# Squares by GpSimd in one leg of a fused attention and feed-forward kernel, and weight rows split earlier

## The chip, the cores and the metric

The kernel runs on one core of a Trainium2 chip. The metric is the device time of one launch in microseconds (us), the median of several runs. A profiled execution gives the trace; its span is the time from the first to the last instruction. Engines: TensorE does the matrix products (PE; PEld for its weight loads), VectorE is DVE, ScalarE ACT, GpSimd POOL, and SyncE (SP) issues the DMAs.

## The reference

Attention with a sink and a window, then a feed-forward layer with squared ReLU (named "moe" in the code, with one expert):

```
scores = q @ k.T / 8                     # 4 batches, 8 heads, 768 positions, head size 64
keep   = (key < 4) or (0 <= query - key < 128)
a      = softmax(where(keep, scores, -1e9))
x      = (a @ v), heads side by side     # 3072 x 512
h      = max(x @ w_in, 0)                # 512 x 2048
out    = (h * h) @ w_out                 # 2048 x 512, float32
```

The weights arrive as float64.

## The kernel before

**Chunks and pairs.** The 3072 tokens form eight chunks of 384 tokens (two a batch), `c` = 0 to 7. Each chunk has four pairs of heads. Attention of a pair makes scores (PE), the masked maximum and exponent (DVE L266, ACT L269), the scaling of the probabilities (GpSimd, `normalise`), transposes (PE, copied by ACT or DVE into PTF), and the values (PE, `xo`), which become x as a high and a low part (ACT L401, DVE L402).

**Precision.** Each float32 operand of the feed-forward products stands as two float32r tiles, high and low, and a product is three products: high·high, low·high, high·low. A weight row (128 x 512 float64) is loaded raw and split into such a pair: `split_steps` runs five DVE instructions (L540, L542, L544, L546, L553), an ACT copy of the low half-words (L539) and an ACT copy that makes the high part (L552). There are NROW = 32 rows, in an order that interleaves four groups of four rows of w_in and four of w_out; HALF is 16. Raw rows take turns in four buffers, and each split issues the load of the row two ahead.

**Legs of products.** `moe` walks through legs (chunk, first and last block of d_ff). Chunks 0 and 1 go through blocks 0 to 7 first (legs 1 and 2), then through 8 to 15 (legs 3 and 4); all other chunks take 16 blocks at a time. For each block, PE adds up 12 products into the PSUM tile `ph` (L448), ACT makes r = ReLU(ph) (L456) and gh = r² rounded to float32r (L459), and DVE makes the square in full (L461, in place in `ph`) and its low part gl = square − gh (L465). While that happens PE does the second products of the block before, nine with 512 columns (L478). The generator yields four times a block; one such step is a quantum. At the end of a leg, `evacuate` copies or adds three PSUM tiles (L496 to L506) and stores them.

**The order.** Leg 1, with the attention of chunks 0 and 1 and the splits of rows 0 to 15, is written out by hand: in that section each engine's instructions keep the program's order. `fill(n)` there does n steps of the splits (five steps make a row), up to HALF rows. From leg 2 on a planner orders each engine's instructions by priority and by its own cost estimates, and moves work ahead where an engine would idle. What it is given is program order: in each leg, `plan` says up to which unit of attention the leg goes, from which row to which row the splits go, and over which share of the leg (the last number). Rows are also split early enough for the blocks that need them (`need`). Leg 2 has no attention units, leg 3 has 24. A split counts as 10 places less urgent than its place in the program.

**Buffers that matter.** `r` has one buffer, `gh` and `gl` two, `ph` two PSUM banks. The probabilities of attention ("P", pool `ap4`) have four buffers of 128 x 792 float32.

Of the kernel before, what the change touches and what calls it, by code (L numbers as in the profile page):

```python
# [8 lines left out]
F32 = mybir.dt.float32  # L9
# [5 lines left out]
ALU = mybir.AluOpType  # L15
# [3 lines left out]
P = 128  # L19
# [4 lines left out]
TOK = 384  # L24
# [11 lines left out]
def f32(ap):  # L36
    return ap.bitcast(F32)
# [3 lines left out]
def sink_window_attention_moe(  # L41
# [11 lines left out]
    nc = tc.nc  # L53
    B, NPAIR, _, S = q.shape
# [12 lines left out]
    with ExitStack() as fast:  # L67
# [5 lines left out]
        ap4 = fast.enter_context(tc.tile_pool(name="ap4", bufs=4))  # L73
# [76 lines left out]
        def wi_at(i, cc, fc):  # L150
            f0 = fc * P
            return wi[:, cc, f0 // WR, i, f0 % WR : f0 % WR + P]
# [81 lines left out]
        def bank(tag, name):  # L234
            pool = {"att": ps_att, "h": ps_h, "xo": ps_x}.get(tag, ps_o)
            return pool.tile([P, 512], F32, tag=tag, name=name)
# [199 lines left out]
        def moe(legs):  # L436

            items = [(c, f0, f1, fc) for c, f0, f1 in legs for fc in range(f0, f1)]
            squares = {}
            for n in range(len(items) + 1):  # L440
                if n < len(items):
                    c, f0, f1, fc = items[n]
                    xh, xl = xT[c]
                    ph = ps_h.tile([P, 512], F32, tag="h", name=f"ph_{c}_{fc}")
                    m = 0
                    for cc in range(NCC):
                        for i, xt in ((0, xh), (1, xh), (0, xl)):
                            nc.tensor.matmul(  # L448
                                ph[:, 0:TOK], wi_at(i, cc, fc), xt[:, cc, :],
                                start=(m == 0), stop=(m == 3 * NCC - 1),  # L450
                            )
                            m += 1
                        if cc % 2 == 1 and cc < NCC - 1:
                            yield
                    r = ap1.tile([P, TOK], F32, tag="r", name=f"r_{c}_{fc}")
                    nc.scalar.activation(r, ph[:, 0:TOK], AF.Relu)  # L456
                    gh = mp.tile([P, TOK], F32R, tag="gh", name=f"gh_{c}_{fc}")
                    gl = mp.tile([P, TOK], F32R, tag="gl", name=f"gl_{c}_{fc}")
                    nc.scalar.activation(gh, r, AF.Square)  # L459
                    yield  # L460
                    nc.vector.tensor_tensor(ph[:, 0:TOK], ph[:, 0:TOK], r, op=ALU.mult)  # L461
                    squares[n] = (gh, gl)
                late = None
                if n < len(items):
                    late = lambda: nc.vector.tensor_tensor(gl, ph[:, 0:TOK], f32(gh), op=ALU.subtract)  # L465
                if n == 0:
                    yield
                    late()
                    yield
                    continue  # L470
                c, f0, f1, f = items[n - 1]
                ghp, glp = squares.pop(n - 1)
                if f == f0:
                    po = [ps_o.tile([P, DM], F32, tag=f"o{t}", name=f"po_{c}_{f0}_{t}") for t in range(NQ)]
                for t in range(NQ):
                    ts_ = slice(t * P, (t + 1) * P)
                    for j, (gt, i) in enumerate(((ghp, 0), (ghp, 1), (glp, 0))):
                        nc.tensor.matmul(  # L478
                            po[t], gt[:, ts_], wo[f][:, i, :],
                            start=(f == f0 and j == 0), stop=(f == f1 - 1 and j == 2),  # L480
                        )
                    if t == 1:
                        yield
                        if late:
                            late()
                if f == f1 - 1:
                    evacuate(c, f0, f1, po)
                yield
# [26 lines left out]
        NROW = len(order)  # L515
        HALF = NROW // 2
# [62 lines left out]
        split = []  # L579

        def row_steps():
            for n in range(NROW):
                yield from split_steps(n)
                split.append(n)
                yield

        FH = NFC // 2
        legs = [(0, 0, FH), (1, 0, FH), (0, FH, NFC), (1, FH, NFC)] + [(c, 0, NFC) for c in range(2, NCHUNK)]
        products = moe(legs)
        QUANTA = 4 * FH  # L590
        with tc.manual_schedule(engines={E.PE, E.DVE, E.Activation, E.Pool, E.SP}):
            steps = row_steps()

            def fill(n):
                for _ in range(n):
                    if len(split) < HALF:
                        next(steps)

            def scores(s, i, tags=("att", "att")):
                for hh in range(2):  # L600
                    score(*pairs[s], hh, i, tags[hh])

            def busy(n):

                t = bank("o2", "idle")
                for _ in range(n):
                    nc.tensor.matmul(t, idle[:, 0:P], idle, start=True, stop=True)

            def tail(s, spare):

                a = pairs[s]
                probs(*a, 0)
                if s == 0:
                    busy(10)
                yield
                sink_keys(*a, spare[0])
                probs(*a, 1, spare[1])
                yield
                probs(*a, 2)
                yield  # L620

            load_qk(*pairs[0])
            load_row(0)
            load_qk(*pairs[1])
            load_row(1)
            load_v(*pairs[0]), load_v(*pairs[1])
            load_row(2)
            split_sinks = load_sinks(0)
            busy(7)

            for s in range(NPAIR + 1):
                if s > 0:
                    load_qk(*pairs[s + 1])
                for i, tags in enumerate((("att", "att"), ("h", "h"), ("o0", "o1"))):
                    scores(s, i, tags)
                    fill(1)
                fill(1)

                normalise(*pairs[s], (0, 1))
                if s == 1:  # L640
                    split_sinks()
                if s < 2:
                    busy(4 + 4 * s)
                rest = values(*pairs[s - 2], True) if s > 1 else None
                if s > 0:
                    if s > 1:
                        load_v(*pairs[s])
                    t = tail(s - 1, ("o2", "h"))
                    next(t)
                    fill(1)  # L650
                    if rest:
                        rest()
                    next(t)
                    fill(1)
                    next(t)
                else:
                    fill(1)
            rest = values(*pairs[NPAIR - 1], True)
            fill(2)
            rest()  # L660

            todo = []
            for s in range(NPAIR + 1, 2 * NPAIR + 1):
                if s < 2 * NPAIR:
                    todo += [lambda s=s: (s + 1 < 2 * NPAIR and load_qk(*pairs[s + 1]), scores(s, 0))]
                    todo += [lambda s=s, i=i: scores(s, i) for i in range(1, NQ)]
                    todo += [lambda s=s: normalise(*pairs[s], (0, 1))]
                else:
                    todo += [lambda: values(*pairs[s - 2])]
                if s > NPAIR + 1:  # L670
                    todo += [lambda s=s: values(*pairs[s - 2])] if s < 2 * NPAIR else []
                t = tail(s - 1, ("att", "att"))
                todo += [lambda t=t: next(t)] * 3
                if s < 2 * NPAIR:
                    todo.append(lambda s=s: load_v(*pairs[s]))
            todo.append(lambda: values(*pairs[2 * NPAIR - 1]))
            for n in range(QUANTA):
                next(products)
                fill(2 if n < QUANTA // 2 and n % 3 or n % 4 == 0 else 1)
                if todo:  # L680
                    todo.pop(0)()
            while len(split) < HALF:
                next(steps)
            for f in todo:
                f()
        nrow = len(split)
# [7 lines left out]
        units, ready = [], [0, 0]  # L694
# [37 lines left out]

        LEAD = 2.5

        plan = [(ready[1], HALF, 24, 1.0), (ready[1] + 24, 24, NROW, 0.9), (ready[2], NROW, NROW, 1.0)]
        plan += [(ready[min(c + 1, NCHUNK - 1)], NROW, NROW, 1.0) for c in range(2, NCHUNK)]
        flag = None
        checked = 0
# [219 lines left out]
```

## Time and profile before

| what | us |
|---|---|
| median of 3 runs (713.13 to 715.03) | 713.21 |
| profiled execution: time | 712.63 |
| profiled execution: span | 710.9 |
| PE busy | 691.0 |
| DVE busy | 486.1 |
| ACT busy | 392.6 |
| POOL busy | 236.4 |

The profile counts an engine as busy while one of its instructions runs; matrix products are pipelined, so a busy PE isn't PE at its peak. In the tables by stage a row has the stretch, its length, and for each engine its busy time with the number of instructions in brackets, then the granted PE clock as a share of full speed, the share of time in which the DMA engines work, and GB/s. A line of a timeline has start, duration, engine, source line, operation and tiles. A group of instructions has count, busy time, mean in ns, then the idle time before them. A wait has the waiting engine and line, what ended the wait, and the total in us, the number of times and the longest.

### The profile page before, as it was taken

The numbers are of one execution on the slowest core, as the hardware profiler recorded it, in microseconds if no ns is written. First come the engines' busy times: TensorE is split into PE (matmuls) and PEld (weight loads), VectorE is DVE, ScalarE is ACT, GpSimd is POOL, SyncE is SP. The second block draws the span as 40 slices with busy tenths as digits, with TensorE's granted clock in tenths as the row PEclk, the third lists the DMA queues.
The fourth block names the chain that finished last, engine by engine and source line by source line (L and its number), as shares of the span: only waits on it lengthen the run. The fifth ranks groups of instructions, "written<-read, shape, count | busy, mean of one in ns | idle before, by whom it ended". The sixth has DMA issues, their size and how long they took to land.

```text
span 710.9 us, 11803 instructions
## 1 busy us (share of the span) xinstructions
PE 691.0 (97%) x3895; PEld 597.2 (84%) x3895; DVE 486.1 (68%) x1275; ACT 392.6 (55%) x1075; POOL 236.4 (33%) x435
## 2 busy tenths in 40 slices
PE   8889999999999999999999999999999999999995
PEld 4567789988878988888898888889888898889995
DVE  8998789996788766665766776665666766542232
ACT  5887666754455666665666666566666443322221
POOL 6655300063455334423324443432443333200000
PEclk9999999999999999999999999999999999999998
DMA  8575345531524433243343523343332310001001
GB/s 241 166 232 168 119 155 175 195 93 27 164 59 129 131 98 102 62 130 106 87 118 103 152 76 94 90 136 109 100 90 83 92 43 16 1 3 43 1 1 49
DMA packets 37013, 71.78 MB, mean 101 GB/s; under 512 B 4368, under 2 KB 14096, under 8 KB 36944
## 3 DMA queue, kind: packets, MB, share of 16 engines
q1 hardware_dynamic: 36944, 70.95, 33.7%
q8 instruction: 33, 0.54, 0.3%
q14 instruction: 36, 0.29, 0.1%
HBM read 63.06 MB, written 7.86 MB: 100 GB/s over the span
## 4 chain that ended last, share of the span: by engine, by line
PE 86%; DVE 6%; ACT 4%; issue 1%; DMA 1%; SPq 1%; DVEq 0%; ACTq 0%
PE po L478 35%; PE ph L448 35%; PE xo L390 6%; PE s L262 4%; PE pt L360 2%; PE xo L393 2%; ACT P L269 1%; PE s L258 1%; PE pss L307 1%; DMA raw<-in_moe_w_in_dram 1%; PE pt L342 1%; DVE gl L465 1%; ACT m L539 1%; DVE ph L461 1%; DVE rs L279 1%
## 5 line engine op out<-in xcount | busy, mean ns | idle before, releaser
L448 PE MATMUL ph<-x,wi 128*128 128x384 f32 x1536 | 306.6, 340 | 0.0
L448 PEld LDWEIGHTS ph<-x,wi 128*128 128x128 f32 x1536 | 265.3, 188 | 8.0 <-issue 1.4
L478 PE MATMUL po<-wo,gh 128*128 128x512 f32 x768 | 244.1, 398 | 0.4 <-DVE ob L497 0.4
L230 POOL TENSOR_TENSOR KS<-kn,KS 128x408 fp32r<-128x408 f32 (+1 forms) x48 | 72.0, 1500 | 330.6 <-DVE KS L229 315.8
L478 PE MATMUL po<-wo,gl 128*128 128x512 f32 x384 | 151.5, 395 | 0.3 <-DVE gl L465 0.3
L478 PEld LDWEIGHTS po<-wo,gh 128*128 128x128 f32 x768 | 135.6, 188 | 18.9 <-issue 1.4
L269 ACT ACTIVATE P<-P,nbs 128x264 f32<-128x264 f32 (+1 forms) x192 | 94.6, 493 | 79.0 <-DVE nbs L266 73.1
L456 ACT ACTIVATE r<-ph 128x384 f32<-128x384 f32 x128 | 62.7, 490 | 111.6 <-PE ph L448 110.9
L461 DVE TENSOR_TENSOR ph<-ph,r 128x384 f32<-128x384 f32 x128 | 71.6, 559 | 63.6 <-ACT r L456 62.7
L266 DVE CUSTOM_DVE_ANT_0 P<-s,masks 128x264 f32<-128x264 f32 x160 | 67.2, 429 | 59.3 <-PE s L262 56.3
L291 POOL TENSOR_SCALAR P<-P,rs 128x136 f32<-128x136 f32 (+2 forms) x192 | 84.2, 454 | 28.6 <-DVE rs L280 13.7
L478 PEld LDWEIGHTS po<-wo,gl 128*128 128x128 f32 x384 | 72.1, 188 | 16.7 <-DVE gl L465 0.8
L465 DVE TENSOR_TENSOR gl<-ph,gh 128x384 fp32r<-128x384 f32 x128 | 71.0, 555 | 10.2 <-DVE ph L461 0.5
L459 ACT ACTIVATE gh<-r 128x384 fp32r<-128x384 f32 x128 | 67.2, 525 | 3.5
L262 PE MATMUL s<-KS,QS 128*128 128x264 f32 (+1 forms) x288 | 57.1, 281 | 0.2
L262 PEld LDWEIGHTS s<-KS,QS 128*128 128x128 f32 x288 | 51.8, 188 | 5.9 <-DVE nbs L266 1.5
L366 DVE TENSOR_TENSOR PTF<-pt,halves 128x256 f32<-128x256 f32 x96 | 36.2, 419 | 22.5 <-PE pt L360 22.0
L279 DVE TENSOR_SCALAR rs<-sm 128x3 f32<-128x3 f32 (+1 forms) x56 | 48.5, 866 | 3.0 <-ACT P L269 1.6
L390 PE MATMUL xo<-PTF,vn 128*64 128x256 f32 x448 | 47.3, 348 | 2.5 <-ACT PTF L349 2.5
L286 POOL TENSOR_TENSOR P<-P 128x256 f32<-128x256 f32 (+1 forms) x48 | 42.9, 894 | 16.7 <-ACT P L269 16.7
L390 PEld LDWEIGHTS xo<-PTF,vn 128*64 128x64 f32 x448 | 31.9, 138 | 19.3 <-issue 9.5
L401 ACT CAST x<-xo 128x384 fp32r<-128x384 f32 x32 | 15.3, 478 | 55.7 <-PE xo L393 55.7
(97 smaller groups left out, 645.9 us busy)
## 6 DMA issues: line engine op xcount, KB each, us to landing
raw<-in_moe_w_in_dram SPq DMA_DIRECT2D x16, 512.0 KB, 4.5
raw<-in_moe_w_out_dram SPq DMA_DIRECT2D x16, 512.0 KB, 3.5
half<-in_moe_w_in_dram SPq DMA_DIRECT2D x32, 256.0 KB, 3.3
half<-in_moe_w_out_dram SPq DMA_DIRECT2D x32, 256.0 KB, 3.4
kn<-in_k_dram SPq DMA_DIRECT2D x24, 272.0 KB, 4.2
qn<-in_q_dram SPq DMA_DIRECT2D x32, 192.0 KB, 3.1
out_dram<-ob SPq DMA_DIRECT2D x24, 256.0 KB, 2.3
kn<-in_k_dram SPq DMA_DIRECT2D x24, 204.0 KB, 3.5
```

Source lines behind the costliest of these rows:

```text
L230: nc.gpsimd.tensor_tensor(KS[:, 1, 0:nk], st["kn"][:, hh, 0:nk], f32(KS[:, 0, 0:nk]), op=ALU.subtract)
L262: nc.tensor.matmul(ps[:, 0:n], st["QS", hh][:, qcols], flat[:, a, c0 : c0 + n], start=(a == 0), stop=(a == 1))
L266: nc.vector.tensor_tensor_reduce(Pt[:, i, 0:n], ps[:, 0:n], mask[:, 0:n], -SCALE, BIG, ALU.add, ALU.min, nb)
L269: nc.scalar.activation(Pt[:, i, 0:n], Pt[:, i, 0:n], AF.Exp, bias=nb, scale=-1.0, accum_out=sm[:, i : i + 1])
L291: nc.gpsimd.tensor_scalar(Pt[:, j, 0:n], Pt[:, j, 0:n], rs[:, hh, j : j + 1], 1.0, op0=ALU.mult, op1=ALU.mult)
L390: nc.tensor.matmul(xo[h * D : h * D + D, cols], lhsT, rhs, start=(n == 0), stop=False, skip_group_check=True)
L448: nc.tensor.matmul(ph[:, 0:TOK], wi_at(i, cc, fc), xt[:, cc, :], start=(m == 0), stop=(m == 3 * NCC - 1),)
L456: nc.scalar.activation(r, ph[:, 0:TOK], AF.Relu)
L459: nc.scalar.activation(gh, r, AF.Square)
L461: nc.vector.tensor_tensor(ph[:, 0:TOK], ph[:, 0:TOK], r, op=ALU.mult)
L465: late = lambda: nc.vector.tensor_tensor(gl, ph[:, 0:TOK], f32(gh), op=ALU.subtract)
L478: nc.tensor.matmul(po[t], gt[:, ts_], wo[f][:, i, :], start=(f == f0 and j == 0), stop=(f == f1 - 1 and j == 2),)
```

## The change

Three things. In leg 2, (c, f0) == (1, 0), GpSimd computes the square from r into a new SBUF tile `sq` and the low part from it; the tile takes turns in the buffers of the probabilities. In the part written by hand two more rows are split (EARLY = 18 instead of 16), and `fill` does two steps in each of the last twelve quanta of leg 1 instead of one or two. In the plan, leg 2 goes from the rows done (18) to 28 instead of from 16 to 24, and leg 3 from 28 to 32 over half of it instead of from 24 to 32 over nine tenths.

```diff
                     nc.scalar.activation(gh, r, AF.Square)
+
+                    spare = (c, f0) == (1, 0)
+                    if spare:
+                        sq = ap4.tile([P, TOK], F32, tag="P", name=f"sq_{c}_{fc}")
+                        nc.gpsimd.tensor_tensor(sq, r, r, op=ALU.mult)
                     yield
-                    nc.vector.tensor_tensor(ph[:, 0:TOK], ph[:, 0:TOK], r, op=ALU.mult)
+                    if not spare:
+                        sq = ph[:, 0:TOK]
+                        nc.vector.tensor_tensor(sq, sq, r, op=ALU.mult)
                     squares[n] = (gh, gl)
                 late = None
                 if n < len(items):
-                    late = lambda: nc.vector.tensor_tensor(gl, ph[:, 0:TOK], f32(gh), op=ALU.subtract)
+                    minus = nc.gpsimd if spare else nc.vector
+                    late = lambda: minus.tensor_tensor(gl, sq, f32(gh), op=ALU.subtract)
...
         QUANTA = 4 * FH
+        EARLY = HALF + 2
...
-                    if len(split) < HALF:
+                    if len(split) < EARLY:
                         next(steps)
...
-                fill(2 if n < QUANTA // 2 and n % 3 or n % 4 == 0 else 1)
+                fill(2 if n < QUANTA // 2 and n % 3 or n % 4 == 0 or n >= QUANTA - 12 else 1)
                 if todo:
                     todo.pop(0)()
-            while len(split) < HALF:
+            while len(split) < EARLY:
                 next(steps)
...
-        plan = [(ready[1], HALF, 24, 1.0), (ready[1] + 24, 24, NROW, 0.9), (ready[2], NROW, NROW, 1.0)]
+        plan = [(ready[1], nrow, 28, 1.0), (ready[1] + 24, 28, NROW, 0.5), (ready[2], NROW, NROW, 1.0)]
```

## The prediction

> **What bounds the kernel now.** I read the page first, then busy time by stage, then what TensorE (PE) waited for in each stage, then VectorE (DVE) instruction by instruction in the second leg. The stages below are cut where a leg's first products begin: leg 1 runs to about 97.2 us, leg 2 (chunk 1, first eight blocks of d_ff) to 130.4, leg 3 to 168, leg 4 to 207.
>
> ```profile
> span 710.9 us, 11803 instructions
> PE 691.0 (97%) x3895; PEld 597.2 (84%) x3895; DVE 486.1 (68%) x1275; ACT 392.6 (55%) x1075; POOL 236.4 (33%) x435
> ```
> ```profile
> core 0: us, PE busy (x) PEld busy (x) DVE busy (x) ACT busy (x) POOL busy (x), PEclk, DMA share, GB/s
> 41.00:60.00 19.00, 18.19 (x96) 13.13 (x95) 17.64 (x53) 16.33 (x43) 8.62 (x14) 1.00 0.59 193
> 60.00:77.00 17.00, 16.32 (x97) 12.48 (x95) 14.17 (x40) 12.32 (x31) 7.10 (x12) 1.00 0.34 113
> 77.00:97.20 20.20, 19.89 (x136) 16.52 (x136) 12.40 (x24) 12.05 (x25) 6.85 (x11) 1.00 0.51 156
> 97.20:130.40 33.20, 33.20 (x168) 30.02 (x167) 32.41 (x71) 21.35 (x39) 0.00 (x0) 1.00 0.55 177
> 130.40:168.00 37.60, 36.10 (x192) 32.40 (x191) 34.73 (x86) 21.68 (x50) 13.66 (x17) 1.00 0.36 110
> 168.00:207.00 39.00, 38.00 (x224) 31.87 (x223) 30.36 (x89) 18.32 (x52) 19.66 (x40) 1.00 0.37 103
> ```
> ```profile
> PE pt L360 <- DVE PTF L369: 1.2, 1, 1.2
> PE po L478 <- DVE gl L465: 0.3, 1, 0.3
> ...
> PE po L478 <- DVE ob L497: 0.4, 1, 0.4
> ```
>
> PE sets the end, at full granted clock in all these stages (1.00). The second column of the stage table is what the change can win: PE stands idle 0.81, 0.68 and 0.31 us in the three parts of leg 1, nothing in leg 2, 37.60 − 36.10 = 1.50 us in leg 3 and 1.00 us in leg 4. The waits (first two rows: leg 3; last row: leg 4) all name DVE. DVE is full in leg 2 (32.41 of 33.20) and nearly in leg 3 (34.73 of 37.60), and GpSimd (POOL) does nothing in leg 2. So the largest gain that the waits offer after leg 1 is 1.50 + 1.00 = 2.5 us, and leg 2 itself can't get faster: it has no PE idle time.
>
> What fills DVE in leg 2:
>
> ```profile
> 116.39 0.57 DVE L461 TENSOR_TENSOR ph<-ph,r 128x384 f32<-128x384 f32 x1
> 116.87 0.68 DVE L553 SCALAR_TENSOR_TENSOR wo<-m,eb 128x512 fp32r<-128x512 int32 x1
> 117.47 0.55 DVE L465 TENSOR_TENSOR gl<-ph,gh 128x384 fp32r<-128x384 f32 x1
> 117.93 0.42 DVE L540 TENSOR_SCALAR t<-raw 128x512 int32<-128x512 int32 x1
> 118.27 0.46 DVE L544 TENSOR_SCALAR m<-raw 128x512 uint16<-128x512 uint16 x1
> 118.61 0.68 DVE L542 SCALAR_TENSOR_TENSOR t<-raw,t 128x512 int32<-128x512 int32 x1
> 119.21 0.42 DVE L540 TENSOR_SCALAR t<-raw 128x512 int32<-128x512 int32 x1
> 119.55 0.42 DVE L546 TENSOR_SCALAR eb<-t 128x512 int32<-128x512 int32 x1
> 119.88 0.68 DVE L542 SCALAR_TENSOR_TENSOR t<-raw,t 128x512 int32<-128x512 int32 x1
> ```
> ```profile
> L461 DVE TENSOR_TENSOR ph<-ph,r 128x384 f32<-128x384 f32 x8 | 4.5, 564 | 0.5 <-ACT r L456 0.3
> ...
> L553 DVE SCALAR_TENSOR_TENSOR wi<-m,eb 128x512 fp32r<-128x512 int32 x6 | 4.1, 683 | 0.0
> L553 DVE SCALAR_TENSOR_TENSOR wo<-m,eb 128x512 fp32r<-128x512 int32 x5 | 3.4, 684 | 0.0
> L501 DVE COPY ob<-po 128x512 f32<-128x512 f32 x2 | 1.4, 682 | 0.0
> ```
>
> Durations overlap by about 0.09 us, so what an instruction costs a full engine is the step from its start to the next start: 0.48 for L461 (square), 0.46 for L465 (low part), 0.34 (L540), 0.34 (L544), 0.60 (L542), 0.33 (L546), 0.60 (L553). A split row is the last five: 2.21 us. Eleven rows ended in leg 2 (six and five L553), though the plan asks for eight: the planner pulls rows ahead until DVE is full. The sum agrees: 33.2 less two evacuations (1.2) less 8 × 0.94 for the squares leaves 24.5 us, or 11.1 rows. So 16 + 11 = 27 of 32 rows are ready when leg 3 begins.
>
> **Squares and low parts on GpSimd.** DVE loses 16 instructions in leg 2: 8 × 0.94 = 7.5 us. GpSimd gains 16 of 128x384 with both inputs in SBUF. The nearest group has that shape and costs 1.01 us. What a GpSimd instruction does to DVE beside it is in these rows:
>
> ```profile
> L286 POOL TENSOR_TENSOR P<-P 128x384 f32<-128x384 f32 x24 | 24.2, 1010 | 16.7 <-ACT P L269 16.7
> ```
> ```profile
> 141.67 0.55 DVE L232 TENSOR_TENSOR QS<-qn,QS 64x384 fp32r<-64x384 f32 x1
> ...
> 143.79 0.53 DVE L461 TENSOR_TENSOR ph<-ph,r 128x384 f32<-128x384 f32 x1
> ```
> ```profile
> 257.40 1.33 DVE L232 TENSOR_TENSOR QS<-qn,QS 64x384 fp32r<-64x384 f32 x1
> ```
> ```profile
> 257.29 1.03 POOL L286 TENSOR_TENSOR P<-P 128x384 f32<-128x384 f32 x1
> ```
> ```profile
> 67.96 1.28 DVE L540 TENSOR_SCALAR t<-raw 128x512 int32<-128x512 int32 x1
> ```
> ```profile
> 143.12 1.26 POOL L286 TENSOR_TENSOR P<-P 128x256 f32<-128x256 f32 x1
> ```
> ```profile
> 166.96 0.73 POOL L286 TENSOR_TENSOR P<-P 128x256 f32<-128x256 f32 x1
> ```
>
> L232 needs 0.55 us; beside a 128x384 GpSimd instruction it took 1.33, so it stood still for 0.78. L540, the first step of a split, took 1.28 instead of 0.42 at 67.96. L461, which reads PSUM, kept its 0.53 while GpSimd worked (143.12 to 144.38). And GpSimd loses a turn in its own way: 1.26 against 0.73. So instructions of the split and GpSimd's exclude each other, while the squares that DVE gives up were of the kind that nobody blocks. Leg 2's DVE is then left with splits alone, and each new GpSimd instruction shuts it out for 0.78 us: 16 × 0.78 = 12.5 us against 7.5 freed. This is the term that speaks against the change: DVE loses 5.0 us in leg 2. Bounds: 0 us, where GpSimd's work fell only beside evacuations and idle moments, and 16 × 1.01 = 16.2, where the whole instruction shuts DVE out. I take 12.5, since DVE is full with splits there.
>
> [...]
>
> GpSimd's own lateness: can the low part reach PE in time?
>
> ```profile
> 115.86 0.49 ACT L456 ACTIVATE r<-ph 128x384 f32<-128x384 f32 x1
> ```
> ```profile
> 120.08 0.19 PEld L478 LDWEIGHTS po<-wo,gl 128*128 128x128 f32 x1
> ```
>
> r is there at 116.35, and PE first loads gl of that block at 120.08, 3.73 us later. Two GpSimd instructions take 2.02, so 1.7 us are over. One lost turn costs 1.26 − 0.73 = 0.53 us, two lost turns in each instruction (0.60 for L553 and 0.34 for L540 right behind it) 2 × 0.94 = 1.9. I take one turn each, 1.1 us: hidden, with 0.6 us to spare, cost 0. If PE's cover is gone, each of eight blocks pays. No wait is added on DVE or ACT: ACT's square gh is ready before GpSimd's first instruction ends, r's single buffer is free 2 to 3 us later (a block takes 33.2 / 8 = 4.15), and ph, which is released earlier now, has nobody waiting (PE idle 0 in leg 2). The new tile sq takes turns with the four probability buffers, which attention doesn't use in leg 2. GpSimd's queue was empty there (x0), so nothing stands behind the squares.
>
> **Two more rows in leg 1.**
>
> ```profile
> L539 ACT COPY m<-raw 128x512 uint16<-128x512 uint16 x6 | 4.7, 779 | 0.0
> ...
> L552 ACT CAST wi<-t 128x512 fp32r<-128x512 f32 x3 | 1.9, 623 | 0.0
> ```
>
> Rows 16 and 17 move from leg 2 into the order written by hand: ten DVE instructions (4.4 us), four ACT ones (copies at L539 and L552), and the loads of rows 18 and 19 are issued on SP in that order too. The new fill rule puts the additions in leg 1's last twelve quanta. There (77 to 97.2) DVE has 12.40 of 20.20 us; with 4.4 it is 83% full, as it was in 60 to 77 (14.17 of 17.00). There PE stood 4.0% idle, in 77 to 97.2 1.5%. I take the difference, 2.5% of 20.2: +0.5 us. Bounds: 0 (steps fall into DVE's gaps) and, if the ACT copies stood on the path one after the other, 2 × (0.78 + 0.62): +2.8. The two loads go beside others: DMA is 0.51 busy there and was 0.59 in the first part; taken as 0.
>
> **The later rows.** In legs 2 and 3 DVE's sum is −4.4 (two rows fewer) − 7.5 + 12.5 = +0.6 us, or nothing within the error. In rows: leg 2 has 33.2 − 1.2 − 12.5 = 19.5 us for splits, 8.8 rows, so 18 + 8.8 = 26.8 are ready when leg 3 begins, against 27. The plan's 28 won't be reached. Rows 28 to 31 asked for in leg 3's first half rather than over all of it change little, since the rows ran ahead of the plan anyway. Leg 3's 1.50 us stay: 0 (−1.5 to +4, if the whole 3.7 + 0.6 us of the upper bound are passed on to PE).
>
> **Sum.** 0 + 0.5 + 0 = +0.5 us. The profiled execution (712.63 us, span 710.9) becomes 713.1; the median of the runs is 0.6 above it, so 713.7.
>
> **Rivals.**
> Faster: GpSimd's squares fall beside DVE's evacuations and gaps, the lock costs little, and DVE is relieved by up to 12 us over legs 2 and 3. Then the waits of legs 3 and 4 go (−1.5 − 1.0), and if leg 1 hides its rows the time is 710.7. For it: DVE waits are all that PE waits for there. Against it: the 1.33 and 1.28 us rows, and a DVE that has only blockable work left.
> Slower: GpSimd comes late with gl. It decides from the point where it loses 0.85 us in each of its two instructions; a full DVE can do that (0.94 for two turns). With r late too, behind one ACT copy (0.6), PE waits about 0.5 us in each block: 8 × 0.5 = 4 us, so 713.7 + 4 = 717.7. Against it: 0.6 us to spare at the one turn measured.
> Nothing happens: the planner already pulls rows ahead of the plan, so the plan's numbers move none of them: 713.2, inside the forecast's case.
>
> **How the numbers follow.** 0.3% is 2.1 us, about what a measurement can tell from no change. Forecast and "nothing happens" together 0.50, with a range of their own from 712.0 to 715.3; faster 0.27 (mostly just over the bound); slower 0.23. The range from 710.6 to 717.0 takes in the faster case and most of the slower one.
>
> **What would show it.** In the profile after: GpSimd busy about 16 us or more in leg 2, with 16 instructions of over 1.0 us each; L540 to L553 longer in the mean there; eight to nine L553 in leg 2 instead of eleven; PE idle in leg 2 near zero (the slower case: waits of po on a GpSimd gl); in 77 to 97 a few tenths more PE idle; in leg 3 still about 1.5 us. The prediction is wrong if ten or more rows end in leg 2 with leg 3's waits gone, or if PE waits for gl in every block.

## The result, and the profile after

The changed kernel takes 725.32 us (median of 6 runs, 721.32 to 728.30) against 713.38 us (6 runs, 712.05 to 715.03) for the kernel before on the same chip: ratio 1.0159, 95% interval 1.0134 to 1.0184. It is about 12 us slower; the forecast was 713.7 with a range up to 717.0. The profiled execution took 728.30 us, span 726.5, against 712.63 and 710.9; it is the slowest of the six, 3 us above their median. Line numbers below are those of the changed kernel: square `sq` L464, low part `gl` L473, split steps L547 to L561, products L486, copies out of `po` L507 (ACT) and L509 (DVE).

The page's first rows, stretches cut at the times at which the stages began before the change, and what PE waited for between 95 and 170 us:

```profile
span 726.5 us, 11824 instructions
...
PE 697.3 (96%) x3895; PEld 601.6 (83%) x3895; DVE 483.9 (67%) x1259; ACT 393.6 (54%) x1075; POOL 263.0 (36%) x451
```
```profile
core 0: us, PE busy (x) PEld busy (x) DVE busy (x) ACT busy (x) POOL busy (x), PEclk, DMA share, GB/s
77.00:97.20 20.20, 19.89 (x137) 16.40 (x135) 17.65 (x36) 14.93 (x31) 7.92 (x11) 1.00 0.51 159
97.20:130.40 33.20, 26.34 (x123) 23.15 (x122) 29.66 (x56) 17.83 (x31) 18.04 (x10) 0.90 0.58 186
130.40:168.00 37.60, 32.46 (x152) 28.65 (x151) 21.27 (x50) 17.36 (x37) 15.85 (x13) 0.91 0.21 69
```
```profile
PE po L486 <- POOL gl L473: 9.9, 2, 5.8
PE po L486 <- DVE ob L509: 1.1, 1, 1.1
PE po L486 <- ACT ob L507: 1.0, 1, 1.0
```

The last part of leg 1 is as before (19.89 of 20.20 us). In the stretch behind it, where PE had no idle time, it has 33.20 − 26.34 = 6.9 us, and in the next 5.1 in the place of 1.5. Nearly all of both is leg 2's: leg 3's first products begin at 146.57 us now, at 130.4 before. Cut there, leg 2 has 10.9 us of idle time and leg 3 has 1.1:

```profile
97.20:146.50 49.30, 38.40 (x173) 33.40 (x172) 40.45 (x76) 27.02 (x47) 29.55 (x16) 0.89 0.45 144
146.50:185.60 39.10, 38.00 (x195) 34.36 (x194) 21.89 (x57) 15.33 (x38) 11.00 (x19) 0.96 0.20 59
```
```profile
146.57 3.51 PE L448 MATMUL ph<-x,wi 128*128 128x384 f32 x12
```

Two waits for GpSimd's low part, both in leg 2, make 9.9 us. GpSimd's timeline shows where they come from; of its 16 instructions these seven, and beside the longest of them DVE and ACT:

```profile
101.01 0.95 POOL L464 TENSOR_TENSOR sq<-r 128x384 f32<-128x384 f32 x1 [14.63 <-ACT r L456]
...
106.59 2.20 POOL L464 TENSOR_TENSOR sq<-r 128x384 f32<-128x384 f32 x1 [3.47 <-ACT r L456]
...
116.32 7.18 POOL L464 TENSOR_TENSOR sq<-r 128x384 f32<-128x384 f32 x1 [3.93 <-PE po L486]
123.58 1.00 POOL L473 TENSOR_TENSOR gl<-sq,gh 128x384 fp32r<-128x384 f32 x1
...
135.41 6.87 POOL L464 TENSOR_TENSOR sq<-r 128x384 f32<-128x384 f32 x1 [2.29 <-ACT r L456]
142.37 1.00 POOL L473 TENSOR_TENSOR gl<-sq,gh 128x384 fp32r<-128x384 f32 x1
143.33 0.82 POOL L464 TENSOR_TENSOR sq<-r 128x384 f32<-128x384 f32 x1
```
```profile
116.10 0.68 DVE L561 SCALAR_TENSOR_TENSOR wo<-m,eb 128x512 fp32r<-128x512 int32 x1
116.70 0.68 DVE L550 SCALAR_TENSOR_TENSOR t<-raw,t 128x512 int32<-128x512 int32 x1
117.30 0.46 DVE L552 TENSOR_SCALAR m<-raw 128x512 uint16<-128x512 uint16 x1
117.65 0.40 DVE L554 TENSOR_SCALAR eb<-t 128x512 int32<-128x512 int32 x1
...
122.40 0.42 DVE L548 TENSOR_SCALAR t<-raw 128x512 int32<-128x512 int32 x1
125.27 0.69 DVE L561 SCALAR_TENSOR_TENSOR wi<-m,eb 128x512 fp32r<-128x512 int32 x1 [2.45 <-ACT m L547]
```
```profile
119.67 0.60 ACT L560 CAST wi<-t 128x512 fp32r<-128x512 f32 x1
123.53 0.49 ACT L456 ACTIVATE r<-ph 128x384 f32<-128x384 f32 x1 [3.26 <-POOL sq L464]
```

A square that took 0.82 us while DVE was idle (143.33) takes 7.18. From 116.10 to 122.82 DVE runs split steps one into the next, at their usual durations (0.40 to 0.68 us) and without a gap: it loses nothing, and GpSimd stands the whole time. It ends when DVE stops: the planner laid two rows into one another, ACT's next copy of `m` stands in its queue behind the next `r`, `r` has one buffer, and that buffer is held by the standing square. So DVE runs dry, and the square is done 0.68 us later. PE waits 5.8 us for its low part, up to 124.63. The clock in that time, and behind the second long square:

```profile
118.00:122.00 4.00, 0.80 (x4) 0.35 (x3) 4.00 (x10) 1.33 (x3) 4.00 (x1) 1.00 0.75 204
122.00:128.80 6.80, 4.17 (x11) 3.50 (x12) 4.35 (x9) 3.54 (x6) 4.68 (x4) 0.50 0.37 139
128.80:135.00 6.20, 6.20 (x33) 5.76 (x32) 4.43 (x10) 3.12 (x6) 1.84 (x2) 1.00 0.47 161
142.50:149.30 6.80, 5.88 (x16) 5.21 (x17) 1.35 (x1) 2.53 (x5) 2.66 (x3) 0.50 0.25 77
```

In the two waits, 3.2 and 3.1 us after PE's last product, the granted clock falls to 0.50, and it stays there for 6.8 us, beyond the end of the wait. PE works 4.17 and 5.88 us of these; two products with 512 columns take 0.86 us from start to start there (144.01 to 144.87), 0.46 at 1.00 (134.59 to 135.05), so I estimate that about half of it is lost: 2.1 + 2.9 = 5.0 us. The account of the profiled pair: 12.0 us of waits, less the 1.5 of before's leg 3, plus 5.0 for the clock is 15.5, against 726.5 − 710.9 = 15.6. The starts of the legs agree: the profiled execution is 1.3 us late at leg 1's first ReLU (45.70 against 44.42 us) and 16.9 us at leg 4's first product (185.67 against 168.76), so legs 2 and 3 lose 15.6 us; the 1.3 us are made good behind them.

### The profile page after: what moved, and what is told of

Its sections match the earlier page's. It is cut to its first block, busy times and chain, and to the rows that moved or that the text cites. A ratio compares the mean times of both kernels' runs of the same rounds, so it can differ in the third digit from the quotient of the medians.

```text
span 726.5 us, 11824 instructions
## 1 busy us (share of the span) xinstructions
PE 697.3 (96%) x3895; PEld 601.6 (83%) x3895; DVE 483.9 (67%) x1259; ACT 393.6 (54%) x1075; POOL 263.0 (36%) x451
## 4 chain that ended last, share of the span: by engine, by line
PE 85%; DVE 5%; ACT 4%; POOL 2%; DMA 2%; issue 1%; SPq 0%; POOLq 0%; DVEq 0%; ACTq 0%
PE po L486 34%; PE ph L448 34%; PE xo L390 5%; PE s L262 5%; PE pt L360 2%; POOL sq L464 2%; PE xo L393 1%; ACT P L269 1%; PE s L258 1%; PE pss L307 1%; DVE P L266 1%; DVE t L550 1%; ACT m L547 1%; PE pt L342 1%; DMA part<-ob 1%
## 5 line engine op out<-in xcount | busy, mean ns | idle before, releaser
L486 PE MATMUL po<-wo,gh 128*128 128x512 f32 x768 | 246.1, 401 | 3.1 <-DVE ob L509 1.1
L486 PE MATMUL po<-wo,gl 128*128 128x512 f32 x384 | 153.2, 399 | 9.9 <-POOL gl L473 9.9
L486 PEld LDWEIGHTS po<-wo,gh 128*128 128x128 f32 x768 | 136.6, 190 | 22.5 <-DVE ob L509 1.5
L468 DVE TENSOR_TENSOR ph<-ph,r 128x384 f32<-128x384 f32 x120 | 67.1, 559 | 68.6 <-ACT r L456 67.9
L486 PEld LDWEIGHTS po<-wo,gl 128*128 128x128 f32 x384 | 72.8, 190 | 26.9 <-POOL gl L473 10.8
L473 DVE TENSOR_TENSOR gl<-ph,gh 128x384 fp32r<-128x384 f32 x120 | 66.6, 555 | 10.0
L231 ACT CAST QS<-qn 64x384 fp32r<-64x384 f32 x48 | 24.6, 512 | 35.8 <-PE s L262 34.7
```

The lines of the kernel that those rows point to most:

```text
L468: nc.vector.tensor_tensor(sq, sq, r, op=ALU.mult)
L473: late = lambda: minus.tensor_tensor(gl, sq, f32(gh), op=ALU.subtract)
L486: nc.tensor.matmul(po[t], gt[:, ts_], wo[f][:, i, :], start=(f == f0 and j == 0), stop=(f == f1 - 1 and j == 2),)
```

## The experiments

All ratios are to the kernel before on the same chip, with 95% intervals. Two theories stood at the start. Standing: a GpSimd instruction that meets an old, unbroken run of DVE instructions stands until it ends. Turns, as in the prediction: each lets the other in after one instruction, and the loss is DVE's time or the two rows.

### Which part of the change

Squares and low parts on GpSimd, rows, `fill` and plan as before:

```diff
-        EARLY = HALF + 2
+        EARLY = HALF
...
-                fill(2 if n < QUANTA // 2 and n % 3 or n % 4 == 0 or n >= QUANTA - 12 else 1)
+                fill(2 if n < QUANTA // 2 and n % 3 or n % 4 == 0 else 1)
...
-        plan = [(ready[1], nrow, 28, 1.0), (ready[1] + 24, 28, NROW, 0.5), ...
+        plan = [(ready[1], HALF, 24, 1.0), (ready[1] + 24, 24, NROW, 0.9), ...
```

> Only the squares and low parts of leg 2 on GpSimd; rows and plan as in the kernel before. Starvation theory (a GpSimd instruction that finds DVE in an unbroken run of split instructions stands until the run has a gap or an instruction that reads PSUM): the planner still fills leg 2 with splits, so at least one square in leg 2 takes over 3 us, PE waits for a GpSimd gl in leg 2, and the time is 718 to 727 us. Turn theory (they take turns, a wait is at most 0.94 us): no square over 2 us, 713 to 716 us. Rows theory (the loss comes from rows split earlier and the plan): 712 to 714 us.

Measured: 728.95 us, 1.0215 [1.0184, 1.0246]. Squares of 7.36 and 5.18 us; PE waits 8.9 us for `gl`. GpSimd's part makes the whole loss.

The rows and the plan alone, squares and low parts on DVE (`spare = False`):

> Only the rows: two more rows in leg 1, the denser fill and the new plan; squares and low parts stay on DVE. Starvation theory: no wait on GpSimd in leg 2, leg 3 has up to two rows fewer, 711.5 to 714 us. Rows theory: most of the loss is here, over 720 us. My prediction's terms: +0.5 us in leg 1, and up to 1.5 us won in leg 3 since 18 + 11 = 29 rows are ready when it begins: 712.2 us.

Measured: 715.14 us, 1.0012 [0.9992, 1.0031]: no change that can be told. PE's waits there are for copies:

```profile
PE po L486 <- DVE ob L509: 2.3, 2, 1.2
PE pt L360 <- DVE PTF L369: 0.7, 1, 0.7
```

Only the squares on GpSimd, low parts on DVE (`minus = nc.vector`):

> As the changed kernel, but the low part gl is made by DVE, from the GpSimd square. [...] Starvation theory: a square ends at the latest when DVE reaches gl in its queue, so no square over 3 us, waits of PE under 3 us in sum, 712 to 716 us. If GpSimd were just slow or its start late: squares stay as long as in the changed kernel (7 us) and the time over 720 us.

Measured: 717.46 us, 1.0047 [1.0032, 1.0062]; squares of 0.96 to 2.69 us, no long one. Here DVE has a dependent low part in each block, which breaks its run. The time is 1.5 us above what the standing theory allowed: PE waits 3.0 us for DVE's copies of `po`, and 0.9 us for `gl`.

Only the low parts on GpSimd, the squares on DVE from PSUM into `sq`:

```diff
-                        nc.gpsimd.tensor_tensor(sq, r, r, op=ALU.mult)
+                    nc.vector.tensor_tensor(sq, ph[:, 0:TOK], r, op=ALU.mult)
```

> As the changed kernel, but the square stays on DVE (from PSUM, into the new SBUF tile) and only the low part gl is GpSimd's. Starvation theory: GpSimd's instruction is released by a DVE instruction that reads PSUM, so the run behind it is young; gl takes under 1.5 us in most blocks, and where it doesn't, it stands until DVE's next square at the latest, about 4 us; waits of PE for a GpSimd gl under 3 us, 713 to 717 us. If every GpSimd instruction in leg 2 were at risk alike: a gl of over 5 us, 718 us or more.

Measured: 719.46 us, 1.0077 [1.0053, 1.0102]; one low part took 5.12 us, so it stood 4.1 us, until DVE's next instruction that reads PSUM, and PE waited 4.1 us for `gl` in two places. So it ended where the standing theory puts the end, but the length and the time are those of the second expectation: a low part is at risk, too. Either half costs less than both; both together take from DVE nearly all that breaks its run.

### What lets GpSimd in

Two runs leave out the whole reference and only set GpSimd instructions of 128x384 beside rows of DVE instructions like the splits'. First, GpSimd released some 0.4 to 0.8 us into DVE's run:

> Leaves out the whole reference: measures the disputed wait alone. A run of DVE instructions (10, 20 or 40 in the order of a split row; 20 with one SBUF input; 20 with two; 20 that read PSUM; 21 with a PSUM reader after every seventh; 20 with a one-column memset after every fifth) starts, and while it runs an ACT copy of 64, 192, 320 or 448 columns releases two GpSimd instructions of 128x384. Starvation theory: beside 10, 20 and 40 split instructions the first GpSimd instruction takes up to about 4, 8 and 17 us, beside PSUM readers 1.0, with a PSUM reader after every seventh up to about 3.5. Turn theory: 1.0 to 2.0 us everywhere.

Measured: every GpSimd instruction 0.82 to 1.37 us, beside all kinds, so at most 0.54 us of waiting. Released early it gets in after one instruction; standing didn't appear. Then released later, by more ACT copies ahead of it:

> Leaves out the whole reference. As the first measurement of the wait, but the GpSimd instruction is released later in the run of DVE split instructions: after 1 to 12 ACT copies of 512 columns (about 0.5 us each), beside 40 split instructions; and after 4, 7, 9 and 11 copies beside 50 with one SBUF input, 28 with two, 35 split instructions with a PSUM reader after every seventh and 35 with a one-column memset after every fifth. [...]

GpSimd's timeline in the stretch with 28 two-input DVE instructions back to back ("waitdouble", released after 4, 7, 9 and 11 copies), and ahead of it the last release beside split steps in row order ("waitforty"):

```profile
258.99 1.14 POOL L93 TENSOR_TENSOR waitforty<-e 128x384 f32<-128x384 f32 x1 [20.25 <-ACT e L91]
...
376.80 0.96 POOL L93 TENSOR_TENSOR waitdouble<-e 128x384 f32<-128x384 f32 x1 [18.39 <-ACT e L91]
377.83 1.32 POOL L95 TENSOR_TENSOR nextdouble<-waitdouble,src 128x384 f32<-128x384 f32 x1
398.16 12.79 POOL L93 TENSOR_TENSOR waitdouble<-e 128x384 f32<-128x384 f32 x1 [19.00 <-ACT e L91]
411.03 0.99 POOL L95 TENSOR_TENSOR nextdouble<-waitdouble,src 128x384 f32<-128x384 f32 x1
419.26 11.49 POOL L93 TENSOR_TENSOR waitdouble<-e 128x384 f32<-128x384 f32 x1 [7.24 <-DVE w L56]
...
440.35 10.19 POOL L93 TENSOR_TENSOR waitdouble<-e 128x384 f32<-128x384 f32 x1 [8.54 <-DVE w L56]
```

Each later release stands less by what it came later: all three end with the run. In row order, where a step follows the one it reads and leaves a gap of 0.035 us, nothing stood at any release, though 5 to 14 us had been expected there, if GpSimd gets in only while DVE's run is young. All DVE instructions of the stretch that stood read two inputs in SBUF; in the kernel three of five split steps read one, so the missing gap is what the two cases have in common. Counted over the traces, with a run being DVE's instructions without a gap, those that read PSUM included: an instruction that met a run younger than about 3 us waited 0.54 us at most (the changed kernel's square at 135.41 met one 3.0 us old, begun at 132.39, and stood); of 25 that met an older one on SBUF, with no GpSimd instruction right ahead of them, 20 stood, to its end or to DVE's next instruction on PSUM (0.8 to 12 us), and five got in. An instruction on PSUM let in what waited, but it didn't make the run young: the low part that stood 4.1 us was released 0.25 us after one. Why a young run yields and an old one doesn't these runs don't show.

The two cases side by side: in a turn, before the change, DVE stopped for 0.78 of the 1.03 us of one GpSimd instruction (257.40); in the changed kernel GpSimd, once it stood, stayed out over 15 DVE instructions, the 7.18 us above.

Is it the single `r` buffer that makes the square late? With `r` in the four buffers of the probabilities in leg 2:

```diff
-                    r = ap1.tile([P, TOK], F32, tag="r", ...)
+                    pool, tag = (ap4, "P") if (c, f0) == (1, 0) else (ap1, "r")
+                    r = pool.tile([P, TOK], F32, tag=tag, ...)
```

> As the changed kernel, but r has a place of its own for each block in leg 2 (it takes turns in the same four buffers as the square), so ACT needn't wait for a standing square before it makes the next r, and its copies for the splits go on. In the changed kernel the standing ended when DVE ran out of such copies. Starvation theory: DVE's run goes on longer, the longest square stands longer than 7.2 us (8 to 15), and the time is 725 to 735 us. If the single buffer of r is the cause of the loss: no long squares, 714 to 717 us.

Measured: 728.52 us, 1.0212 [1.0184, 1.024]. ACT and DVE run on, and one square takes longer still, 11.60 us; PE waits 10.1 us at a stretch, to 129.50, and has half the clock for 10.2 us, 6.8 of them still in the wait:

```profile
PE po L487 <- POOL gl L474: 11.8, 2, 10.1
```
```profile
122.70:132.90 10.20, 3.40 (x8) 2.75 (x9) 4.99 (x12) 1.49 (x3) 8.46 (x4) 0.50 0.42 131
```

So the buffer didn't cause the standing, it ended it.

The same GpSimd work in leg 4, where DVE has attention in place of splits (`spare = (c, f0) == (1, FH)`, rows as changed):

> As the changed kernel, but GpSimd has the squares and low parts of leg 4 (chunk 1, last eight blocks) instead of leg 2; the rows as in the changed kernel. In leg 4 DVE has scores, transposed probabilities and evacuations that read PSUM, and no splits. Starvation theory: no GpSimd square over 2 us beside DVE, unless GpSimd's own queue (scaling of probabilities) is ahead of it; 713 to 716 us, as with the rows alone. If GpSimd is late in itself: waits for a GpSimd gl of several us in leg 4, over 718 us.

Measured: 714.51 us, 1.0007 [0.999, 1.0023], GpSimd instructions of 0.88 (squares) and 1.02 us (low parts) in the mean, no wait for `gl`. There the operation did no harm.

### Without standing, and still slow

One buffer for `t` instead of two: the planner can't interleave rows, and dependent steps become neighbours on DVE.

```diff
-            t1 = ap2.tile([P, WR], I32, tag="t1", ...)
+            t1 = ap1.tile([P, WR], I32, tag="t1", ...)
```

> The changed kernel with all its GpSimd work, but with one buffer for t instead of two (the checks' small tile half shares it), so that the planner can't interleave two rows: on VectorE a row's dependent steps become neighbours (t, then eb from t, then the row from eb), as in the micro run, where such neighbours left a gap of 0.035 us and GpSimd never stood. Theory 1 (GpSimd stands behind a run of overlapped VectorE instructions without a gap, once the run is some 3 us old): the gaps return, no square takes over 2.0 us, PE's waits of gl in legs 2 and 3 fall from 9.9 to under 2 us, 714 to 718 us. Theory 2 (it is VectorE's load that keeps GpSimd out, whatever the order of its instructions; VectorE stays as full): squares of 5 to 7 us remain, 722 to 729 us. Theory 3, mine before (turns, and what goes wrong is the work that both share): squares of 1.0 to 1.6 us, but the time stays above 722 us.

Measured: 727.73 us, 1.0194 [1.017, 1.0219]. No instruction of GpSimd's stood, as the standing theory expected; its time was wrong by 10 us. The third theory, turns, had the time (above 722 us), and the squares nearly (0.83 to 1.00 us).

```profile
L473 POOL TENSOR_TENSOR gl<-sq,gh 128x384 fp32r<-128x384 f32 x8 | 9.2, 1154 | 1.4 <-ACT gh L459 0.5 <-POOL sq L464 0.4
L464 POOL TENSOR_TENSOR sq<-r 128x384 f32<-128x384 f32 x8 | 7.1, 882 | 38.5 <-ACT r L456 38.5
```
```profile
PE po L486 <- DVE ob L509: 3.9, 3, 2.0
PE po L486 <- POOL gl L473: 2.1, 3, 0.9
```

Now DVE is the one shut out: 16 of its split steps between 97.2 and 150 us took longer than the shortest of their form, by 10.8 us together (in the changed kernel 8 by 5.9). The control, the same rows and single buffer without GpSimd's work:

> The control to the run with one buffer for t: the change's rows and plan, the squares and low parts on VectorE as before, one buffer for t. It prices the single buffer and the uninterleaved rows by themselves: a gap of 0.035 us two or three times a row and a wait of ACT's copy of t, together 0 to 0.3 us a row, some 14 rows in legs 2 and 3: 715 to 718 us (the same rows with two buffers gave 715.14). All theories agree here; what the run with GpSimd's work gives above this one is what GpSimd costs without interleaved rows.

Measured: 714.75 us, 1.0011 [1.0, 1.0023]. So GpSimd's work costs 13 us here too, with no standing at all.

What is this loss? Four runs on it. Leg 2 without squares and low parts (products read `gh` a third time):

> The changed kernel's rows and plan; in leg 2 neither squares nor low parts are computed by anyone, the products take gh a third time in the place of gl. VectorE is relieved of 7.5 us and GpSimd does nothing there: the best that moving the work away could give. All theories: the waits of leg 2 and most of leg 3's go, 711.5 to 713.5 us.

Measured: 711.34 us, 0.9969 [0.9951, 0.9987]. 3 us is the most that relieving DVE of this work brings. GpSimd's 16 instructions added again, into a tile that nobody reads, with `r` in the buffers of the probabilities:

> As the run that leaves squares and low parts out, but GpSimd does 16 instructions of the same size at the same places (r times r, then minus r) into a tile that nobody reads, r in the four buffers of the probabilities so that ACT doesn't wait for it. What GpSimd takes from VectorE stays, what its lateness does to PE is gone. Theory P (the loss is GpSimd's results coming late to PE): GpSimd's instructions stand as long as before, several us, and the time is 711.5 to 714.5 us all the same. Theory L (the loss is VectorE's, shut out by GpSimd): 718 us or more, PE waiting for copies of po and for ACT.

Measured: 721.99 us, 1.0117 [1.009, 1.0145]. The run isolates less than it was meant to: a square took 11.63 us and held its `r`, and ACT's `r` of the second block behind it had to wait for that buffer, so that PE's longest wait came from the standing by another way:

```profile
128.96 0.49 ACT L459 ACTIVATE r<-ph 128x384 f32<-128x384 f32 x1 [4.32 <-POOL sq L476]
```

The same with one buffer for `t`, where no square stands:

> As the run with unread GpSimd work, with one buffer for t, so that GpSimd takes its turns and VectorE loses some 12 us to them. With the results read this gave 727.7 us. Theory P: 712.5 to 716 us, since 12 us lost against 7.5 freed leave VectorE's splits late by some 4 us that hide in legs 3 and 4. Theory L: 720 us or more: then the single-buffer run's loss is VectorE's lost time.

Measured: 725.09 us, 1.0153 [1.0128, 1.0177]: 10 us above its control by the ratios, though PE reads nothing of GpSimd's and no GpSimd instruction took over 1.34 us. It is DVE's lost time, and ACT and PE show how it arrives:

```profile
140.26 0.78 ACT L552 COPY m<-raw 128x512 uint16<-128x512 uint16 x1 [0.58 <-DVE wo L566]
140.91 0.47 ACT L459 ACTIVATE r<-ph 128x384 f32<-128x384 f32 x1
141.41 0.52 ACT L462 ACTIVATE gh<-r 128x384 fp32r<-128x384 f32 x1
```
```profile
111.29 4.56 PE L491 MATMUL po<-wo,gh 128*128 128x512 f32 x12 [1.99 <-DVE ob L514]
136.34 2.34 PE L491 MATMUL po<-wo,gh 128*128 128x512 f32 x9 [1.54 <-ACT gh L462]
141.99 1.65 PE L491 MATMUL po<-wo,gh 128*128 128x512 f32 x6 [1.19 <-ACT gh L462]
148.42 0.70 PE L491 MATMUL po<-wo,gh 128*128 128x512 f32 x2 [1.51 <-DVE ob L514]
```

The last split step of a row is late on DVE; ACT's copy into the single `m` waits for it; `r` and `gh` of the next block stand behind that copy in ACT's queue; PE waits for `gh`. The copies of `po` stand behind splits in DVE's queue in the same way. Taking these copies off DVE, in the single-buffer kernel with GpSimd's results read:

```diff
-                elif t % 2:
+                elif t % 2 or f1 < NFC:
```

> The changed kernel with one buffer for t (727.7 us) and the copies out of po at the ends of legs 1 and 2 on ACT. If PE's waits of the VectorE copies (3.9 us, and about 1.7 us at half clock behind the longest) add up with the rest: 721 to 723.5 us. If the chain from ACT over GpSimd to gl was late anyway and merely hid behind those copies: 725 to 729 us, with gl waits of 5 us or more.

Measured: 725.29 us, 1.015 [1.0121, 1.0178], about 3 us less by the ratios. The time lies at the lower end of the second expectation; waits for `gl` rise from 2.1 to 4.0 us, less than the 5 it asked for, and PE waits 3.0 us for ACT's copies. The lateness moves from one place to the next.

Does it need a packed DVE? Splits of rows 18 to 31 kept to the plan (18 to 23 in leg 2, the first step of each in program order), GpSimd's work as changed, two buffers for `t`; and the control with squares and low parts on DVE:

```diff
+            if n >= EARLY:
+                tc.keep_in_program_order(first)
-        plan = [(ready[1], nrow, 28, 1.0), (ready[1] + 24, 28, NROW, 0.5), ...
+        plan = [(ready[1], nrow, 24, 1.0), (ready[1] + 24, 24, NROW, 0.9), ...
```

> The changed kernel with all its GpSimd work and two buffers for t, but with the splits paced: leg 2 asks for rows 18 to 23 (leg 3 for 24 to 31), and the first step of each of these rows keeps its place in the program on VectorE, so that the planner can't pull rows ahead. Seven rows fall into leg 2 instead of ten, one behind the other, with idle time between them: VectorE's work there is about 7 x 2.2 + 1.2 = 17 of 33 us, which leaves room for the 12 us of turns. Theory F (the loss is the fixed order of a VectorE packed with pulled-ahead splits: GpSimd stands behind their unbroken run, or shuts them out and the copies, ACT's queue and gl come late): no square over 2 us, PE waits under 3 us in legs 2 and 3, 712.5 to 717 us. Theory L2 (GpSimd beside splits costs some 10 us however much room VectorE has): 722 us or more.

> The control: the paced rows with squares and low parts on VectorE (17 + 7.5 = 25 of 33 us in leg 2). Pacing by itself: the rows not pulled ahead fall into leg 3, where VectorE was busy 34.7 of 37.6 us before, so PE's waits there may grow: 713 to 717 us. What the paced run with GpSimd's work gives above or below this one is what GpSimd's work is worth when VectorE has room: theory F between -2 and +2 us, theory L2 +6 us or more.

Measured: 720.14 us, 1.0083 [1.0061, 1.0105], control 714.27 us, 1.0003 [0.9984, 1.0022]. No square stood, PE had the full clock, and GpSimd's work costs 5.7 us by the ratios in place of 13: neither expectation, between them, with PE's waits at 6 us in sum where the theory of the fixed order allowed 3. The room was there but not where it was needed: the rows ran one behind the other to 129.8, then DVE was idle for 9.7 us, waiting for `r`:

```profile
128.81 0.99 DVE L554 TENSOR_SCALAR m<-raw 128x512 uint16<-128x512 uint16 x1
139.49 0.57 DVE L468 TENSOR_TENSOR ph<-ph,r 128x384 f32<-128x384 f32 x1 [9.70 <-ACT r L456]
```

That room between the rows would bring the loss to nothing wasn't tried.

### The rows with the copies on ACT

The rows and the plan of the change on DVE, with the copies out of `po` of legs 1 and 2 on ACT:

> The change's rows and plan without GpSimd's part, and in addition the copies out of po at the ends of legs 1 and 2 all on ACT, none on VectorE. Theory: PE's waits of the VectorE copy ob (2.3 us, 2 times, at the starts of legs 2 and 3) go, as ACT has 12 of 33 us free in leg 2: 712.5 to 713.8 us, 1.3 to 2.6 below the rows alone (715.14). Rival: ACT, whose copies stand behind the casts of the split and r, is as late as VectorE: 714.5 to 716 us, with the same waits under the name of the ACT copy.

Measured: 713.24 us, 0.9986 [0.9975, 0.9997], the waits for the copies gone. It is the best complete version, by 0.14%, less than the 0.3% that the prediction names as what a measurement can tell. That copy alone in the kernel before:

> The kernel before, with the copies out of po at the ends of legs 1 and 2 all on ACT and nothing else of the change. Before, PE waited 0.4 us for such a copy in leg 4 and 1.2 us for a PTF copy in leg 3, so that little can be won: theory 712.3 to 713.4 us (ratio 0.998 to 1.000). If ACT's copies come late instead: 714 us or more, with PE waits of the ACT copy at the starts of legs 2 and 3.

Measured: 713.82 us, 1.0003 [0.9991, 1.0015]: nothing.

## Why the prediction was wrong

**GpSimd's lateness: the step that failed.** "I take one turn each, 1.1 us: hidden, with 0.6 us to spare, cost 0" rested on one row (1.26 against 0.73 us), taken beside a DVE that read PSUM between its other instructions. Eleven of the 16 instructions of the change took that or less, but three squares took 2.20, 7.18 and 6.87 us. The prediction had seen that DVE "is then left with splits alone" and drew from it only what GpSimd does to DVE; that a run of such instructions shuts GpSimd out for its whole length wasn't among its ends. "No wait is added on DVE or ACT" fell with it: ACT's `r` waited 3.26 us for one standing square and 3.38 us for the other, and DVE's split steps waited behind ACT.

**The slower rival** named the right place and the right wait (po on a GpSimd `gl`), with two mis-sized terms: 0.5 us in each of eight blocks, where it was 5.8 and 4.0 us in two of them; and nothing for the clock, where 6.8 us at 0.50 twice cost some 5 us.

**DVE's 12.5 us.** The price of a turn was nearly right where turns are taken: 10.8 us in the run with one buffer for `t`, for 12.5. In the changed kernel it was 5.9, since DVE's steps kept their 0.40 to 0.68 us while GpSimd stood. What followed from it was wrong: "8.8 rows" would fit into leg 2 and the rest would come later. After the change all 15 rows that were left end before leg 3 begins, ten up to 130.4 us and the last at 145.8: the planner, by its own estimates, had put them into leg 2, and the order of the queues is fixed when the kernel is built. DVE's lost time moves no row to a later leg; it makes everything behind it late, ACT's `r` and the copies of `po` among them. So "+0.6 us, or nothing", a balance of DVE's sums, had no bearing on PE: with the results unread and one buffer for `t` the same balance, −7.5 + 10.6 = +3.1 us, cost 10 us.

**Right:** that PE sets the end, and that no more than about 2.5 us are to be won (the run without squares: 3.1 below the kernel before, 714.43 to 711.34). The two rows cost nothing that can be told (1.0012); their +0.5 us in leg 1 doesn't show (19.89 of 20.20 us in both). "Leg 3's 1.50 us stay" came out at 1.1 us, with the rows alone as after the change, under another name: the waits for PTF and `gl` went, and one for a copy of `po` came. So the rows that were ready earlier won little there.

**The signs that were announced.** 16 instructions of over 1.0 us: twelve were 1.00 or more, but what told was the longest of them. Eight or nine rows in leg 2: fifteen; ten or more was, together with the end of leg 3's waits, one of the signs of being wrong. PE idle near zero in leg 2: 10.9 us, with waits of `po` on `gl`, which the prediction had set down for the slower case, but in two blocks and not in every one.

## What to carry to other kernels

Before work goes to GpSimd, look at what DVE will have left beside it. If that is a long run of instructions on SBUF alone with nothing that reads PSUM and no dependent neighbours, GpSimd may stand until the run ends, as it did for 7.18 us in the kernel and 12.79 in the stretch alone, and a fixed order of queues passes on what DVE loses where they take turns (10.8 us of DVE's, 13 us of time with one buffer for `t`). Price the move at the engine that is relieved (leave the work out: 3 us here), and ask for the wait of the whole chain, not for the sum of an engine's busy time.

## What the runs showed of the hardware

GpSimd stood behind DVE for up to 12.0 us (12.79 less 0.83) in the measured stretch of two-input instructions, and for 6.4 us (7.18 less 0.82) in the changed kernel, while DVE's steps took their usual 0.40 to 0.68 us; where dependent neighbours left a gap of 0.035 us, it got in (0.83 to 1.36 us for the first of the two instructions, at twelve releases).

PE's granted clock fell to a half 3.1 to 3.3 us after PE had stopped, and stayed there for 6.8 us with a wait of 5.8 or 4.0 us, for 10.2 us with one of 10.1. In the run with one buffer for `t` a wait of 2.0 us, ahead of 111.85, was followed by half the clock as well, also some 3 us after its begin (between 112.8 and 113.2 us; PE had stopped at 109.86):

```profile
111.00:113.00 2.00, 1.15 (x5) 0.99 (x6) 2.00 (x4) 1.58 (x4) 0.92 (x1) 1.00 0.46 170
113.00:116.20 3.20, 3.20 (x10) 2.45 (x9) 3.10 (x6) 1.25 (x3) 1.10 (x2) 0.50 0.62 191
116.20:120.00 3.80, 3.80 (x21) 3.52 (x20) 3.52 (x8) 2.76 (x5) 0.81 (x1) 0.97 0.55 158
```

A wait of 2.6 us, in the run with the low parts on DVE, left it at 1.00 in both stretches from 97.2 to 168 us. So the length of a wait alone doesn't tell whether the clock falls; what decides it these runs don't show.
